# Three scatter tables in place of one, and an earlier routing queue, in an attention and mixture-of-experts kernel

## The chip, the cores and the metric

The kernel runs on one core of a Trainium2 chip. The metric is device time in microseconds, the median of several executions. The engines are TensorE (PE; PEld is its loading of weights), VectorE (DVE), ScalarE (ACT), GpSimd (POOL) and SyncE (SP), each with a queue of its own that is worked in order. GpSimd issues the indirect DMAs (gathers and scatters by a list of addresses) and the stores of attention outputs, SyncE the plain loads.

## What is computed

Windowed attention for 8 batches of 8 heads, 576 positions each (half the heads look back 32 positions, half 128 positions in steps of 4), then a mixture of 8 experts with one expert for each of 4608 tokens:

```python
x = attention(q, k, v).transpose(0, 2, 1, 3).reshape(4608, 512)
logits = x @ w_gate                       # 8 experts
expert_idx = argmax(logits, axis=1)
gate_w = softmax(logits)[arange, expert_idx]
for e in range(8):
    mask = expert_idx == e
    out[mask] = gate_w[mask, None] * (maximum(x[mask] @ w1[e], 0) @ w2[e])
```

## The kernel before

**Attention** runs over 36 steps, each a block of 128 rows; nine steps are a pair of batches (`NPR = 4` pairs, numbered 0 to 3 here and called first to last in the text). `step(n)` issues the scores of block n (L264), the transposed probabilities of n-1, the output of n-2 (L311), the normalised rows `xs` (L331, three buffers), their two or three stores to `x_d` on GpSimd (L343, L353), the transposed rows of n-3 and the router's logits of n-4. Loads of queries, keys and values run three to five steps ahead on SyncE, six buffers each.

**Routing** (`route(m)`) is called once a pair. It puts its operations into the list `side`, from which `pull_off` takes one at five places of a step, and `pull_pe` those for TensorE, if at least `GAP` pulls have gone by since the last one or the step is `FREE` or later. It picks the expert by argmax (`mx`, `sh`, `cand`, `fst`, `oh`), counts ranks with three matmuls (`rank`), and makes for each token a slot in a table of 40960 integers, held by expert and then by place; `at_i` is the slot's address. `scatter` (L502) then writes the tokens' row numbers to the table `t_d` in device memory by nine indirect DMAs of 128 integers. As all write the one tensor, each waits for the one before.

The first two pairs (`EARLY = 2`) are enough for two blocks of expert 0: `early_fetch` reads two columns of the table into `row_i` (L616), gathers 2 x 128 rows (L683), and `turn_x` (L731) transposes them in later attention steps. After the third pair the whole table is read into `tbl`. The last pair needs no scatter: `mark` makes two one-hot tiles for each of nine blocks (`s1`, L514, and `b1`, L523; every third `b1` on GpSimd), `enter` multiplies them on TensorE into `tb` (L534), and `row_i = tbl + scr` (L603) is the whole list of rows. The stretch from the last attention step to the first gathers with it is called the seam.

**Experts**: 8 static blocks of 4 x 128 rows, and dynamic blocks for what is left, split float32 matmuls in two layers (L771, L802), weights loaded by SyncE and GpSimd and split by ScalarE and VectorE (L657, L658).

**Order.** For steps 0 to 34 (`MEND = 35`) TensorE, VectorE and ScalarE keep the order of the code; later steps, GpSimd and SyncE are ordered by the scheduler of the framework, which also sets the waits between engines. Which work a step holds is set by `at(n, ...)`: route(m) is due after step 13, 22, 31 (five after the pair's last block) and 39.

Of the kernel before, what the change touches and what calls it, by code (L numbers as in the profile page):

```python
# [9 lines left out]
F32 = mybir.dt.float32  # L10
F32R = mybir.dt.float32r
I32 = mybir.dt.int32
BF16 = mybir.dt.bfloat16
AF = mybir.ActivationFunctionType
ALU = mybir.AluOpType
# [9 lines left out]
DM = H * DH  # L25
NE = 8
DF = 1024
P = 128
# [4 lines left out]
NPR = B // 2  # L33
S2 = 2 * S
NT = S2 // P
# [8 lines left out]
NBK = NE * BPE  # L44
# [4 lines left out]
DUMMY = P  # L49
# [5 lines left out]
EB = 2  # L55

NTHR = 40
NWARM = 9
GAP, FREE = 4, 31

# [8 lines left out]
def _constants():  # L69
    c = np.zeros((P, C_ALL), np.float32)  # L70
# [25 lines left out]
    end = row[:, -1].astype(np.float32) - LAST  # L96
    slots = np.repeat(np.arange(P, dtype=np.int32), NBK).reshape(P, NBK)

# [9 lines left out]
    mask = mask.astype(mybir.dt.np(BF16))  # L108
    return dict(cst=c, tok=tok, end=end, slots=slots, mask=mask, zero=np.zeros((DUMMY, DM), np.float32))

# [37 lines left out]
@with_exitstack  # L148
def attention_moe_kernel(ctx, tc, qk, v, wg, w, cst, tok, end, slots, mask, zero, out):
    nc = tc.nc  # L150
# [6 lines left out]
    g_d = dram.tile([N + DUMMY, 1], F32, name="g_d")  # L157
    t_d = dram.tile([P * NBK, 1], I32, name="t_d")

    cc = const.tile([P, C_ALL - C_ATT], F32, name="cc")  # L160
    ident = const.tile([P, P], F32, name="ident")
    crun = const.tile([P, NE], F32, name="crun")
    tbl = const.tile([P, NBK], I32, name="tbl")
    scr = const.tile([P, NBK], F32, name="scr")
# [53 lines left out]
    def load_rest():  # L218
        nc.sync.dma_start(cc, cst[:, C_ATT:])
        nc.sync.dma_start(rows_i, tok)  # L220
        nc.sync.dma_start(rows_f, end)
        nc.sync.dma_start(t_d[:].rearrange("(p b) o -> p (b o)", p=P), slots)

# [190 lines left out]
    def off_pe(f, *a, **k):  # L414
        side.append((0, lambda: f(*a, **k)))
# [16 lines left out]
    def route(m, then=None, after=None):  # L432


        v = nc.vector
        lgs = lgts[m]
        box = {}

# [18 lines left out]
        def small(name, shape=(P, NT, NE), dt=F32):  # L457
            return sp.tile(list(shape), dt, name=name, bufs=1)
# [6 lines left out]
        ]  # L465
        pos, blk_i, plc_i, at_i = [
            small(n, (P, NT), I32) for n in ("pos", "blk_i", "plc_i", "at_i")
        ]
# [25 lines left out]
        def gate_out():  # L494
            nc.scalar.copy(gts, box["gt"])
            taken[0] = False
            lo = DUMMY + m * S2
            nc.sync.dma_start(g_d[lo : lo + S2].rearrange("(t p) o -> t (p o)", p=P), gts)

        def scatter(ts):  # L500
            for t in ts:
                nc.gpsimd.indirect_dma_start(  # L502
                    out=t_d[:],
                    out_offset=bass.IndirectOffsetOnAxis(ap=at_i[:, t : t + 1], axis=0),
                    in_=rows_i[:, m, t : t + 1],
                    in_offset=None,
                )
# [3 lines left out]
        def mark(t):  # L511
            s1 = sp.tile([P, P], F32R, name="s1", bufs=6)
            b1 = sp.tile([P, NBK], F32R, name="b1", bufs=6)
            v.tensor_scalar(  # L514
                s1,
                ca[:, C_IO - C_TRI : C_IO + P - C_TRI],
                plc[:, t : t + 1],
                pay[:, t : t + 1],
                op0=ALU.is_equal,
                op1=ALU.mult,  # L520
            )
            e = v if t % 3 else nc.gpsimd
            e.tensor_scalar(  # L523
                b1, cc[:, C_BK - C_ATT : C_BK + NBK - C_ATT], blk[:, t : t + 1], None, op0=ALU.is_equal
            )
            hot[t] = s1, b1
# [43 lines left out]
        off_pe(v.tensor_copy, pos, posf)  # L570
        off_pe(v.tensor_scalar, blk_i, pos, -P, None, op0=ALU.bitwise_and)
        if m < NPR - 1:
            off_pe(v.tensor_scalar_mul, wide, posf, float(NBK))
            off_pe(
# [11 lines left out]
        else:  # L586
            off_pe(v.tensor_scalar, plc_i, pos, P - 1, None, op0=ALU.bitwise_and)
            off_pe(v.tensor_copy, blk, blk_i)
# [24 lines left out]

    def read_table(to, n):

        nc.sync.dma_start(to[:, :n], t_d[:].rearrange("(p b) o -> p (b o)", p=P)[:, :n])  # L616

# [364 lines left out]
    def at(n, f, *a):  # L982
        todo.setdefault(n, []).append(lambda: f(*a))

    turning = []

    def early_fetch():
        def fetch():
            at(now[0] + 1, read_table, row_i, EB)
            at(now[0] + 2, first.fetch_x)  # L990
            for i in range(EB):
                at(now[0] + 3 + 2 * i, turning.append, i)

        off_pe(fetch)

    def early_gates():
        off_pe(lambda: at(now[0] + 2, first.fetch_gates))
        reserve()

    now = [0]  # L1000
    for m in range(NPR):
        last = (m + 1) * NT - 1 + (4 if m == NPR - 1 else 5)
        if m == EARLY - 1:
            at(last, route, m, early_fetch, early_gates)
        elif m == NPR - 2:
            at(last, route, m, lambda: off_pe(read_table, tbl, NBK))
        else:
            at(last, route, m)
# [332 lines left out]
_HOST = ["q", "k", "v", "moe_w_gate", "moe_w1", "moe_w2"]  # L1341
_ARGS = ["qk", "v", "wg", "w", "cst", "tok", "end", "slots", "mask", "zero"]

# [22 lines left out]
```

## Time and profile before

| | |
|---|---|
| median of 3 runs | 692.63 us (690.27 to 693.84) |
| profiled execution | 692.2 us, of it 690.2 us span |
| TensorE busy | 622.8 us, 90% |
| VectorE busy | 355.7 us, 52% |
| ScalarE busy | 308.3 us, 45% |
| GpSimd busy | 276.8 us, 40% |

TensorE is the engine that sets the time over most of the span; the question for a change is where it isn't busy. "Idle before" of a row is the time in which the engine had nothing to run just ahead of it, with the engine or transfer that ended it. The granted clock of TensorE is given as a share of full speed, which has two levels, 1.2 and 2.4 GHz; a stretch between them is a mixture.

### The profile page before, as it was taken

How to read it: one execution, taken by the hardware profiler on the slowest of the kernel's cores; microseconds unless marked ns; L12 is line 12 of the kernel's file. 1: busy time of each engine (PE TensorE's matmuls, PEld its weight loads, DVE VectorE, ACT ScalarE, POOL GpSimd, SP SyncE). 2: the span in 40 equal slices, each digit the busy share in tenths (PEclk: the TensorE clock that was granted, in tenths of full speed). 3: DMA queues.
4: the chain of work that ended last, by engine and by line, in shares of the span. 5: the costliest groups of instructions: out<-in, count | busy, mean ns of one | idle time of the engine just before them, and what ended most of it. 6: DMA issues, size and time to landing. Idle time of an engine off the chain costs nothing. (4 is left out here: it accounts for less than half of the span.)

```text
span 690.2 us, 13243 instructions
## 1 busy us (share of the span) xinstructions
PE 622.8 (90%) x5231; PEld 497.8 (72%) x5231; DVE 355.7 (52%) x756; ACT 308.3 (45%) x610; POOL 276.8 (40%) x316
## 2 busy tenths in 40 slices
PE   7999996794296889999999999999999999999991
PEld 6777775673275767888888878878887888778781
DVE  3877874574064694656445635744563661361210
ACT  2676673373072343555445535633553551351100
POOL 0333333566454564413630661473165155323220
PEclk8999999799599799999999999999999999999996
DMA  8999997782221355737627744663764465454310
GB/s 330 409 411 399 369 340 235 220 267 85 76 70 40 94 193 180 240 114 246 209 94 239 232 155 145 218 215 85 252 214 153 168 223 208 143 213 156 115 43 32
DMA packets 42183, 135.09 MB, mean 196 GB/s; under 512 B 9204, under 2 KB 10136, under 8 KB 42072
## 3 DMA queue, kind: packets, MB, share of 16 engines
q1 hardware_dynamic: 21608, 75.72, 31.1%
q0 software_dynamic: 20512, 58.51, 25.6%
q8 instruction: 42, 0.69, 0.4%
q14 instruction: 21, 0.17, 0.1%
HBM read 114.91 MB, written 19.99 MB: 195 GB/s over the span
## 5 line engine op out<-in xcount | busy, mean ns | idle before, releaser
L771 PE MATMUL hps<-x,wu 128*128 128x512 f32 (+1 forms) x720 | 168.7, 390 | 3.2 <-DVE h L783 2.8
L658 DVE TENSOR_TENSOR wu<-raw,wu 128x512 fp32r<-128x512 f32 x200 | 128.6, 687 | 80.0 <-ACT wu L657 76.8
L802 PE MATMUL yps<-wu,h 128*128 128x512 f32 x696 | 166.7, 394 | 0.0
L771 PEld LDWEIGHTS hps<-x,wu 128*128 128x128 f32 x720 | 134.0, 191 | 32.4 <-DVE h L783 4.0
L802 PEld LDWEIGHTS yps<-wu,h 128*128 128x128 f32 x696 | 129.8, 188 | 29.7 <-issue 0.6
L657 ACT CAST wu<-raw 128x512 fp32r<-128x512 f32 x200 | 113.0, 618 | 82.3 <-DMA raw<-in_w_dram,wi 39.2
L703 POOL DMA_INDIRECT out_dram<-y,row_i x32 | 35.1, 1096 | 136.2 <-DVE y L702 88.2
L301 ACT COPY pts<-pt 96x512 f32<-96x512 f32 x72 | 42.0, 583 | 89.0 <-PE pt L296 78.3
L783 DVE SCALAR_TENSOR_TENSOR h<-hps,h 128x512 fp32r<-128x512 f32 (+1 forms) x60 | 39.5, 669 | 76.4 <-ACT h L782 68.5
L782 ACT ACTIVATE h<-hps 128x512 fp32r<-128x512 f32 (+1 forms) x60 | 34.2, 582 | 95.9 <-PE hps L771 72.1
L835 POOL DMA_INDIRECT raw<-in_w_dram,wi x40 | 42.6, 1066 | 41.8 <-DVE wu L658 30.9
L275 DVE TENSOR_REDUCE nm<-s 128x4 f32<-128x384 f32 x72 | 39.5, 549 | 35.0 <-PE s L264 32.3
L683 POOL DMA_INDIRECT xg<-x_d,row_i x32 | 33.8, 1056 | 50.9 <-PE tpx L826 25.0
L311 PE MATMUL o<-vr,pts 96*64 96x65 f32 x1152 | 43.3, 230 | 8.2 <-DVE xs L331 8.1
L296 PE MATMUL pt<-ident,p 128*96 128x128 f32 x288 | 48.9, 295 | 1.6 <-ACT pts L301 1.6
L343 POOL DMA_DIRECT2D x_d<-xs x36 | 20.7, 574 | 71.8 <-DVE xs L331 38.8
L311 PEld LDWEIGHTS o<-vr,pts 96*64 96x64 f32 x1152 | 38.2, 142 | 15.6 <-DVE xs L331 9.1
L883 PE MATMUL ypd<-wu,hd 128*128 128x512 f32 x168 | 46.5, 415 | 0.3 <-ACT hd L872 0.3
L502 POOL DMA_INDIRECT t_d<-rows_i,at_i x27 | 27.4, 1014 | 47.3 <-DMA t_d<-rows_i,at_i 38.4
L702 DVE TENSOR_SCALAR y<-yps,gate 128x256 f32<-128x256 f32 x30 | 14.4, 481 | 56.1 <-ACT y L701 56.1
L280 DVE TENSOR_TENSOR d<-s,nm 128x384 f32<-128x384 f32 x72 | 40.0, 557 | 4.8
L701 ACT ACTIVATE y<-yps,gate 128x256 f32<-128x256 f32 x30 | 14.2, 473 | 62.5 <-PE yps L802 58.7
(160 smaller groups left out, 766.3 us busy)
## 6 DMA issues: line engine op xcount, KB each, us to landing
raw<-in_w_dram SPq DMA_DIRECT2D x64, 512.0 KB, 4.9
qkr<-in_qk_dram SPq DMA_DIRECT2D x36, 576.0 KB, 8.1
vr<-in_v_dram SPq DMA_DIRECT2D x36, 520.0 KB, 5.4
x_d<-xs POOLq DMA_DIRECT2D x44, 128.0 KB
x_d<-xs POOLq DMA_DIRECT2D x8, 112.0 KB
x_d<-xs POOLq DMA_DIRECT2D x8, 96.0 KB
x_d<-xs POOLq DMA_DIRECT2D x8, 80.0 KB
raw<-in_w_dram,wi POOLq DMA_INDIRECT x40
```

The source lines that it names most:

```text
L275: nc.vector.tensor_reduce(st["nm", n][:, g], st["s", n][g], axis=AX.X, op=ALU.max)
L280: nc.vector.tensor_tensor(st["d", n][:, g], st["s", n][g], st["nm", n][:, g].broadcast_to([P, HP, KB]), op=ALU.subtract,)
L296: nc.tensor.transpose(pt[:KB, h], st["p", n][:, g, h], ident)
L301: nc.scalar.copy(st["pts", n][:, g], st.pop(("pt", n))[:KB])
L311: nc.tensor.matmul(st["o", n][QB * j : QB * (j + 1), g, h], lhsT=pts[:, g, h, QB * j : QB * (j + 1)], rhs=vr[:KB, n % NRV, a : a + DH + 1] ...
L657: nc.scalar.copy(u[:, 0, sl], raw[:, sl])
L658: nc.vector.tensor_tensor(u[:, 1, sl], raw[:, sl], u[:, 0, sl].bitcast(F32), op=ALU.subtract)
L771: nc.tensor.matmul(hps[:, : self.ns], lhsT=u[:, wpart, fs], rhs=self.x[:, xpart, c, : self.ns], start=(k == 0), stop=(k == 11),)
L783: nc.vector.scalar_tensor_tensor(h[:, 1, :n], hps[:, :n], 0.0, h[:, 0, :n].bitcast(F32), op0=ALU.max, op1=ALU.subtract,)
L802: nc.tensor.matmul(yps, lhsT=self.h[f][:, hpart, ts], rhs=u[:, wpart, fs], start=(k == 0), stop=(k == 23),)
L835: nc.gpsimd.indirect_dma_start(out=raw, out_offset=None, in_=w, in_offset=bass.IndirectOffsetOnAxis(ap=self.wi[:, u : u + 1], axis=0),)
L883: nc.tensor.matmul(yps, lhsT=self.h[f // 4][:, hpart, f % 4], rhs=u[:, wpart, fs], start=(k == 0), stop=(k == 23),)
```

## The change

- There are three tables, `tabs`, cleared to zero; the scatter of block t goes to table t % 3, and what it writes is `rel_i`, the row number less the place in the block (`plc_i`), so that an empty slot is zero.
- Reading is three DMAs into `tbl`, `scr` and `none` (`read_table`), and `add_tables` adds them and the place, two VectorE operations. For the early read the addition and the gathers are due three steps after the step that takes the last scatter from the list; before, the gathers were due two steps after it.
- All `b1` one-hots of the last pair are on VectorE, and the copy of each pair's gates goes from ScalarE to VectorE.
- The routing of the first three pairs is due one step earlier (after steps 12, 21 and 30), `GAP` is 3 in place of 4, `FREE` 35 in place of 31, and the first TensorE operation of a routing waits for the gap too.

```diff
-GAP, FREE = 4, 31
+GAP, FREE = 3, 35
...
-    t_d = dram.tile([P * NBK, 1], I32, name="t_d")
+    tabs = [dram.tile([P * NBK, 1], I32, name=f"tab{i}") for i in range(3)]
...
-        nc.sync.dma_start(t_d[:].rearrange("(p b) o -> p (b o)", p=P), slots)
+        for tab in tabs:
+            nc.sync.dma_start(
+                tab[:].rearrange("(p b) o -> p (b o)", p=P), zero[:, :NBK].bitcast(I32)
+            )
...
+        ticks[1] = ticks[0] - 1
...
-            nc.scalar.copy(gts, box["gt"])
+            v.tensor_copy(gts, box["gt"])
...
-                    out=t_d[:],
+                    out=tabs[t % 3][:],
                     out_offset=bass.IndirectOffsetOnAxis(ap=at_i[:, t : t + 1], axis=0),
-                    in_=rows_i[:, m, t : t + 1],
+                    in_=rel_i[:, t : t + 1],
...
-            e = v if t % 3 else nc.gpsimd
-            e.tensor_scalar(
+            v.tensor_scalar(
...
+        off_pe(v.tensor_scalar, plc_i, pos, P - 1, None, op0=ALU.bitwise_and)
         if m < NPR - 1:
+            off_pe(v.tensor_tensor, rel_i, rows_i[:, m], plc_i, op=ALU.subtract)
...
-    def read_table(to, n):
-
-        nc.sync.dma_start(to[:, :n], t_d[:].rearrange("(p b) o -> p (b o)", p=P)[:, :n])
+    parts = [tbl, scr, none]
+
+    def read_table(n):
+
+        for tab, to in zip(tabs, parts):
+            nc.sync.dma_start(
+                to[:, :n].bitcast(I32), tab[:].rearrange("(p b) o -> p (b o)", p=P)[:, :n]
+            )
+
+    def add_tables(to, n):
+
+        t0, t1, t2 = [t[:, :n] for t in parts]
+        nc.vector.scalar_tensor_tensor(
+            t0,
+            t0.bitcast(I32),
+            cc[:, C_P - C_ATT : C_P + 1 - C_ATT],
+            t1.bitcast(I32),
+            op0=ALU.add,
+            op1=ALU.add,
+        )
+        nc.vector.tensor_tensor(to[:, :n], t0, t2.bitcast(I32), op=ALU.add)
...
+    def read_all():
+        off_pe(read_table, NBK)
+        off_pe(add_tables, tbl, NBK)
+
     def early_fetch():
         def fetch():
-            at(now[0] + 1, read_table, row_i, EB)
-            at(now[0] + 2, first.fetch_x)
+            at(now[0] + 1, read_table, EB)
+            at(now[0] + 3, add_tables, row_i, EB)
+            at(now[0] + 3, first.fetch_x)
             for i in range(EB):
-                at(now[0] + 3 + 2 * i, turning.append, i)
+                at(now[0] + 4 + 2 * i, turning.append, i)
...
-        last = (m + 1) * NT - 1 + (4 if m == NPR - 1 else 5)
+        last = (m + 1) * NT - 1 + 4
```

The order of instructions shows what moves. GpSimd, at the scatters of the first pair, before (x_d rows are the stores of attention outputs; the names behind "waits" are counters of other engines and of GpSimd's own eight DMA counters in turn, the first of them mostly that of the DMA eight before, a second one that of the scatter waited for):

```order
L502 DMA t_d<-rows_i,at_i 40960x1 [waits DMAHW0_49,DMAHW2_49,DMASW0_49,DVE_49]
L343 DMA x_d<-xs 128x256 [waits DMASW1_49,DVE_49]
L353 DMA x_d<-xs 128x256 [waits DMASW2_49]
L502 DMA t_d<-rows_i,at_i 40960x1 [waits DMASW3_49,DMASW0_49]
L502 DMA t_d<-rows_i,at_i 40960x1 [waits DMASW4_49,DMASW3_49]
L343 DMA x_d<-xs 128x256 [waits DMASW5_49,DVE_49]
L353 DMA x_d<-xs 128x256 [waits DMASW6_49]
L502 DMA t_d<-rows_i,at_i 40960x1 [waits DMASW7_49,DMASW4_49]
```

and the same place of the changed kernel:

```order
L505 DMA tab_65<-rel_i,at_i 40960x1 [waits DMAHW2_49,DMASW0_49,DVE_49]
L505 DMA tab_66<-rel_i,at_i 40960x1 [waits DMAHW3_49,DMASW1_49]
L505 DMA tab_67<-rel_i,at_i 40960x1 [waits DMAHW4_49,DMASW2_49]
L505 DMA tab_65<-rel_i,at_i 40960x1 [waits DMASW3_49,DMASW0_49]
L505 DMA tab_66<-rel_i,at_i 40960x1 [waits DMASW4_49,DMASW1_49]
L505 DMA tab_67<-rel_i,at_i 40960x1 [waits DMASW5_49,DMASW2_49]
L345 DMA x_d<-xs 128x256 [waits DMASW6_49,DVE_49]
L355 DMA x_d<-xs 128x256 [waits DMASW7_49]
L505 DMA tab_65<-rel_i,at_i 40960x1 [waits DMASW3_49]
```

Each scatter waited for the one before; now it waits for the third before, and six stand ahead of the next store in place of one.

VectorE in the seam, before, from the gathered logits of the last pair (`lt`) on:

```order
L453 TENSOR_REDUCE lt<-tl 128x24 x2
L415 TENSOR_REDUCE mx<-lt 128x9
L542 TENSOR_TENSOR sh<-lt,mx 128x72
L544 SCALAR_TENSOR_TENSOR cand<-sh,ca 128x72
L546 TENSOR_REDUCE fst<-cand 128x9
```

and in the changed kernel:

```order
L456 TENSOR_REDUCE lt<-tl 128x24 x2
L629 SCALAR_TENSOR_TENSOR tbl<-tbl,cc,scr 128x320
L804 SCALAR_TENSOR_TENSOR x<-s,x 128x256
L456 TENSOR_REDUCE lt<-tl 128x24
L417 TENSOR_REDUCE mx<-lt 128x9
L637 TENSOR_TENSOR tbl<-tbl,none 128x320
L544 TENSOR_TENSOR sh<-lt,mx 128x72
L546 SCALAR_TENSOR_TENSOR cand<-sh,ca 128x72
L548 TENSOR_REDUCE fst<-cand 128x9
```

The two additions over the whole tables have moved in between the operations of the last pair's routing.

SyncE, from the last loads of attention on, in the changed kernel (before, one read `row_i<-t_d` and one `tbl<-t_d` stood there):

```order
L196 DMA vr<-in_v_dram 128x1040 x2
L772 DMA raw<-in_w_dram 128x1024
L622 DMA tbl<-tab_65 128x2
L501 DMA g_d<-gts 9x128
L622 DMA scr<-tab_66 128x2
L622 DMA none<-tab_67 128x2
L196 DMA vr<-in_v_dram 128x1040
L772 DMA raw<-in_w_dram 128x1024 x3
L622 DMA tbl<-tab_65 128x320
L622 DMA scr<-tab_66 128x320
L501 DMA g_d<-gts 9x128
L622 DMA none<-tab_67 128x320
```

Each read has become three, with one load of values and weights behind the first three.

## Rows read from the trace of the kernel before

**Rows 1.** Busy time by stage: length, then busy and count by engine, clock, DMA.

```profile
core 0: us, PE busy (x) PEld busy (x) DVE busy (x) ACT busy (x) POOL busy (x), PEclk, DMA share, GB/s
...
18.50:98.20 79.70, 79.70 (x1547) 61.80 (x1546) 62.58 (x156) 53.96 (x115) 29.17 (x52) 1.00 1.01 387
98.20:152.10 53.90, 43.56 (x744) 33.04 (x742) 30.20 (x82) 28.30 (x62) 28.02 (x40) 0.91 0.77 250
152.10:197.00 44.90, 21.22 (x342) 16.52 (x341) 15.26 (x41) 14.87 (x32) 22.63 (x27) 0.77 0.27 89
...
270.00:677.40 407.40, 403.70 (x1991) 325.73 (x1989) 194.12 (x317) 177.24 (x333) 152.78 (x147) 1.00 0.53 175
```

**Rows 2.** Timeline of TensorE: scores of steps 13, 22, 26, 27, 31, 35.

```profile
59.43 0.89 PE L264 MATMUL s<-qkr 64*64 64x96 f32 x32
...
98.24 0.89 PE L264 MATMUL s<-qkr 64*64 64x96 f32 x32
...
124.41 1.37 PE L264 MATMUL s<-qkr 64*64 64x96 f32 x32
...
130.28 0.89 PE L264 MATMUL s<-qkr 64*64 64x96 f32 x32
...
152.11 0.89 PE L264 MATMUL s<-qkr 64*64 64x96 f32 x32
...
197.01 0.89 PE L264 MATMUL s<-qkr 64*64 64x96 f32 x32
```

**Rows 3.** Timeline of all engines: the two long waits in attention.

```profile
119.22 0.69 DVE L331 TENSOR_TENSOR xs<-o,rz 128x512 f32<-128x512 f32 x1 [7.50 <-DMA x_d<-xs]
...
179.70 0.33 SPq L616 DMA_DIRECT2D row_i<-t_d  x1
182.25 1.00 POOL L683 DMA_INDIRECT xg<-x_d,row_i  x1 [4.95 <-DMA row_i<-t_d]
...
185.83 1.08 PE L731 MATMUL tpx<-ident,xg 128*128 128x128 f32 x4 [20.52 <-DMA xg<-x_d,row_i]
```

**Rows 4.** Timeline of GpSimd: scatters, a weight subtraction, a gather.

```profile
101.09 1.01 POOL L502 DMA_INDIRECT t_d<-rows_i,at_i  x1 [4.45 <-DMA t_d<-rows_i,at_i]
...
166.84 1.28 POOL L672 TENSOR_TENSOR wu<-raw,wu 128x512 fp32r<-128x512 f32 x1
...
170.78 0.97 POOL L502 DMA_INDIRECT t_d<-rows_i,at_i  x1 [1.46 <-DMA t_d<-rows_i,at_i]
...
183.56 0.98 POOL L683 DMA_INDIRECT xg<-x_d,row_i  x1 [0.30 <-issue]
...
204.54 0.99 POOL L502 DMA_INDIRECT t_d<-rows_i,at_i  x1 [2.86 <-DMA t_d<-rows_i,at_i]
```

**Rows 5.** Timeline of all engines in the seam.

```profile
198.42 0.17 DVE L415 SCALAR_TENSOR_TENSOR at_i<-blk_i,wide 128x9 int32<-128x9 int32 x1
...
214.04 0.23 DVE L542 TENSOR_TENSOR sh<-lt,mx 128x72 f32<-128x72 f32 x1
...
217.40 0.38 DVE L523 TENSOR_SCALAR b<-cc,blk 128x320 fp32r<-128x320 f32 x1
...
219.83 0.38 DVE L523 TENSOR_SCALAR b<-cc,blk 128x320 fp32r<-128x320 f32 x1
...
226.13 0.64 PE L534 MATMUL tb<-b,s 128*128 128x320 f32 x1 [8.11 <-POOL b L523]
...
234.95 0.48 DVE L415 TENSOR_TENSOR row_i<-tbl,scr 128x320 int32<-128x320 int32 x1
...
240.10 0.66 PE L826 MATMUL tpx<-ident,xg 128*128 128x128 f32 x4 [0.61 <-DMA xg<-x_d,row_i]
```

**Rows 6.** Page, groups: the first store of each attention output.

```profile
L343 POOL DMA_DIRECT2D x_d<-xs x36 | 20.7, 574 | 71.8 <-DVE xs L331 38.8
```

**Rows 7.** Page, DMA issues: loads of values, median to landing.

```profile
vr<-in_v_dram SPq DMA_DIRECT2D x36, 520.0 KB, 5.4
```

More of the change, by code (lines that the diff above doesn't have):

```diff
@@ L96, in _constants @@
     end = row[:, -1].astype(np.float32) - LAST
-    slots = np.repeat(np.arange(P, dtype=np.int32), NBK).reshape(P, NBK)
     t, p, w = np.meshgrid(np.arange(NT), np.arange(P), np.arange(KB), indexing="ij")
@@ L108, in _constants @@
     mask = mask.astype(mybir.dt.np(BF16))
-    return dict(cst=c, tok=tok, end=end, slots=slots, mask=mask, zero=np.zeros((DUMMY, DM), np.float32))
+    return dict(cst=c, tok=tok, end=end, mask=mask, zero=np.zeros((DUMMY, DM), np.float32))
 def _layout(q, k, v, wg, w1, w2):
@@ L148, in attention_moe_kernel @@
 @with_exitstack
-def attention_moe_kernel(ctx, tc, qk, v, wg, w, cst, tok, end, slots, mask, zero, out):
+def attention_moe_kernel(ctx, tc, qk, v, wg, w, cst, tok, end, mask, zero, out):
     nc = tc.nc
@@ L162, in attention_moe_kernel @@
     crun = const.tile([P, NE], F32, name="crun")
-    tbl = const.tile([P, NBK], I32, name="tbl")
+    tbl = const.tile([P, NBK], F32, name="tbl")
     scr = const.tile([P, NBK], F32, name="scr")
@@ L465, in route @@
         ]
-        pos, blk_i, plc_i, at_i = [
-            small(n, (P, NT), I32) for n in ("pos", "blk_i", "plc_i", "at_i")
+        pos, blk_i, plc_i, at_i, rel_i = [
+            small(n, (P, NT), I32) for n in ("pos", "blk_i", "plc_i", "at_i", "rel_i")
         ]
@@ L586, in route @@
         else:
-            off_pe(v.tensor_scalar, plc_i, pos, P - 1, None, op0=ALU.bitwise_and)
             off_pe(v.tensor_copy, blk, blk_i)
@@ L985, in attention_moe_kernel @@
     turning = []
+    def read_all():
+        off_pe(read_table, NBK)
+        off_pe(add_tables, tbl, NBK)
     def early_fetch():
         def fetch():
-            at(now[0] + 1, read_table, row_i, EB)
-            at(now[0] + 2, first.fetch_x)
+            at(now[0] + 1, read_table, EB)
+            at(now[0] + 3, add_tables, row_i, EB)
+            at(now[0] + 3, first.fetch_x)
             for i in range(EB):
-                at(now[0] + 3 + 2 * i, turning.append, i)
+                at(now[0] + 4 + 2 * i, turning.append, i)
         off_pe(fetch)
     def early_gates():
-        off_pe(lambda: at(now[0] + 2, first.fetch_gates))
+        off_pe(lambda: at(now[0] + 3, first.fetch_gates))
         reserve()
@@ L1005, in attention_moe_kernel @@
         elif m == NPR - 2:
-            at(last, route, m, lambda: off_pe(read_table, tbl, NBK))
+            at(last, route, m, read_all)
         else:
@@ L1341 @@
 _HOST = ["q", "k", "v", "moe_w_gate", "moe_w1", "moe_w2"]
-_ARGS = ["qk", "v", "wg", "w", "cst", "tok", "end", "slots", "mask", "zero"]
+_ARGS = ["qk", "v", "wg", "w", "cst", "tok", "end", "mask", "zero"]
 def kernel(**inputs):
```

## The prediction

> **What bounds the kernel now.** I read the busy time by stage first, then the start of every attention step on TensorE, then the longest waits, then the queue of GpSimd, and last the seam where attention hands over to the experts.
>
> By stage [rows 1] TensorE is never idle from 18.5 to 98.2 us, and nearly never from 270 to 677.4 us (403.7 of 407.4 us busy). Between them it is not: 43.6 of 53.9 us busy, then 21.2 of 44.9 us, and in both the granted clock is below one. So whatever shortens 98 to 240 us moves the rest forward as it is, and nothing else in the change can pay.
>
> The step starts [rows 2] give the undisturbed pace. From step 13 (59.43) to step 22 (98.24) nine steps and the routing of one whole pair take 38.81 us, 4.31 us a step. The next nine take 53.87 us (152.11), and the four after that 44.90 us (197.01) where four undisturbed ones would take 17.2. That is 42.7 us over the pace in 13 steps.
>
> The waits name the cause [rows 3]. At 119.22 VectorE had waited 7.5 us for an attention output buffer whose store to memory was stuck on GpSimd's queue. At 185.83 TensorE had been idle 20.52 us in front of the transposes of the first expert's rows: their gather waited for the table (read issued at 179.70, gather at 182.25), and the read waited for the last of 18 scatters. The scatters are chained [rows 4]: each goes to the same table and waits for the one before. With loads streaming, GpSimd stood 4.45 us behind a scatter of 1.02 us, a pitch of 5.47 us; with the queues quiet 1.46 us behind one, 2.48 us; near the end of attention 2.86, or 3.88 us. Two gathers to different tiles follow each other with 0.30 us between, so a pitch near 1.3 us is what GpSimd can issue.
>
> **The change part by part.** *Three tables.* Scatter t now waits for scatter t-3 only, as the order of GpSimd in the section on the change shows. Nine scatters become three rounds. I take the loaded 5.47 us for a round, as loads still stream when they run: 16.4 us instead of nine pitches, 49 us. The Trainium skill ("DMA: Bandwidth & Descriptors", section on the anatomy of one DMA on the gpsimd path) puts the fixed cost of such a DMA at about 2.0 us, whatever the load; with the 1.02 us of issue that is 3 us a round. The quiet pitch agrees with it, the loaded one doesn't, and I go by the loaded one.
>
> First pair, steps 13 to 22 and beyond: the nine scatters are out in about 14 us, GpSimd's stores of attention outputs stand behind at most six scatters (some 8 us), and an output buffer comes round again after three steps (12.9 us at the pace). The wait of 7.5 us and the smaller ones after it mostly go. I leave 1.2 us of them; 0 and 4 are the bounds. Steps 22 to 31 then take 38.81 + 1.2 = 40.0 us, step 31 starts at 138.3 instead of 152.11: a gain of 13.9 us. In it lie the half-speed steps after each idle stretch: the scores of step 26 (124.41) took 1.37 us, and that step, to 130.28, 5.87 us, some 1.5 over the pace [rows 2]. The gates' copies on VectorE instead of ScalarE are a part of the pace and cost nothing: one short copy each, on an engine with slack.
>
> Second pair: here the chain is still the one that ends last. Its first scatter leaves about 6 us after the start of step 27 (the addresses are the third routing operation of that step). Three rounds, 16.4 us, follow, and two subtractions of weights of 1.28 us [rows 4] stand between scatters on GpSimd; the rounds have room for about half of them, so 1.5 us. Then the last scatter's own landing is included in the third round, and three small reads follow, 2.55 us as the one at 179.70 took [rows 3]. The sum of tables is possible some 27 to 29 us after the start of step 27; I take 28.5, with the stores of step 26 wedged in. What was a wait of TensorE for the gather becomes a wait of VectorE: the two additions stand ahead of the maxima of step 32, which VectorE would begin five steps (21.6 us) and about 1 us for the scores after step 27. So VectorE stands for 28.5 - 22.6, about 6 us, with all of attention behind it on that engine, and TensorE follows through the scores' buffers. I price it at 6.5 us and the lower clock after it at 1.5 us (as in step 26). Bounds: at the quiet pitch the chain is 9 us shorter and the wait is gone; at 7 us a round it is 4.6 us longer. SyncE stands in front of the reads meanwhile, but all loads of queries and keys are ahead of them; only one load of values (needed at step 37) and weights are behind.
>
> Steps 31 to 35 then cost 17.2 + 0.7 (one transposition of gathered rows that the pace doesn't hold; 1.08 at the lower clock [rows 3]) + 6.5 + 1.5 = 25.9 us. Step 35 starts at 138.3 + 25.9 = 164.2 instead of 197.01: **32.8 us gained**.
>
> *The seam.* Before, the third pair's addresses were ready 1.4 us after the scores of step 35; its table is read late, and nothing waits for it. The last pair's chain ran: first operation after the maxima at 214.04, one-hots from 217.40, first product with them at 226.13 after TensorE had waited 8.11 us for two one-hots that GpSimd had behind its scatters, the row list at 234.95, the first transposes of gathered rows at 240.10, 43.1 us after step 35 [rows 5]. Now GpSimd's one-hots go to VectorE. From 217.40 to 219.83 nine starts took 2.43 us, so 18 cost 18 x 0.27 = 4.9 us, and the 8.11 us go. But two things are put in front. The third pair's ranking now stands behind the scores of step 35, not ahead of them: its addresses come one step later, 1.4 + 4.3 + 0.7, about 6.5 us after step 35. And the addition of the three tables stands on VectorE inside the last pair's chain. Nine scatters at 1.3 us and five stores at 0.57 us between them [rows 6] are 14.6 us; the last lands 3.9 - 1.3 us later, at +23.7; the read of a whole table (160 KB) lies between the small one, 2.55 us, and a 520 KB load, 5.4 us [rows 7], say 3.4: +27.1. VectorE would have been there at +17, so it waits 10 us. From there as before: 3.4 us to the one-hots, 4.9 us of them, 0.5 us to the last product, then the 3.1 us of passes over the sum, the row list at +39, against +38.4 before (234.95 + 0.48). The one-hots' gain is eaten by the tables: **0.6 us lost**, between 5 lost (loaded pitch, slow reads) and 4.5 gained (quiet pitch).
>
> *Small things.* Two more tables to clear are 320 KB more on queues full from 18.5 to 98.2 us, but TensorE didn't stand once there. Four VectorE operations more a pair, under 0.2 us each, lie in VectorE's slack (62.6 of 79.7 us busy [rows 1]). From 270 us on nothing changes.
>
> **Sum.** The profiled execution took 692.2 us (span 690.2, 2.0 around it), 0.4 below the median, so no correction. 692.2 - 32.8 + 0.6 = **660.0**.
>
> **The rivals.** (1) *The quiet pitch holds even under load*: rounds of 2.5 to 3 us. Then VectorE never waits at the additions of step 31 (8.0 us more gained), the first pair's rest goes (1.2) and the seam gains up to 3: 660 - 12, about 648. For it: the quiet rows, and the page's 2 us. Against it: the loaded rows are of just this stage. By that page's figure this is the case that comes.
> (2) *Scatters in flight slow each other*: three at once take about 11 us a round. The second pair's chain ends 16 us later, on VectorE, the seam 5: about 681. For it: all go through one queue, among stores and loads. Against it: gathers issued 1.3 us apart show no wait for each other.
> (3) *They don't overlap at all*, in that the queue finishes one scatter before it starts the next. This is the case that ends slower. The chains are then as long as before and attention gains nothing but the gates' copies (some 3 us); in the seam, nine scatters at 3.88 us from +6.5 end at +41.4, the read at +44.8, the row list at +56.7 where it was +38.4: 18 lost, 692 - 3 + 18, about 707. Attention gaining only 3 us, it decides against the change once the row list comes later than +41.4, which is when the nine take over some 20 us in the seam. Against it: the same rows of gathers.
> That the change doesn't do what it says (waits still on the one before) is shut out by the order of GpSimd.
>
> **How the numbers follow.** My forecast 0.78, rival 1 0.11, rival 2 0.07, rival 3 0.04. Its own range: 660 less 8.0, 1.2 and 3 is 648, plus 4.6, 2.8 and 4.5 is 672. That holds most of rival 1 and leaves out the other two, so the range is 647 to 672. A measurement of this kernel can tell about 0.5% (3.5 us) from no change: faster 0.95, the same 0.01, slower 0.04.
>
> **What would show it.** Right: step 22 still near 98 and step 31 near 138; scatters 1.3 us apart in threes with some 2.5 us between the threes; one idle stretch of 4 to 9 us on VectorE ahead of the table's addition near 143 us; step 35 near 164; in the seam VectorE idle about 10 us ahead of the second addition and no wait for one-hots; the stage from the first gathered rows to the end as long as now. Wrong: step 31 well past 140 (stores still starve buffers), scatters over 6 us a round, or a seam that differs from 43 us by over 5.

## The result and the profile after

The changed kernel takes 671.8 us (median of four runs, 668.6 to 675.0) beside 691.8 for the one before: a ratio of 0.971, 95% interval 0.965 to 0.976. That is faster, and 0.2 us inside the stated range of 647 to 672, but 20 us are gained where 32 were forecast. The profiled execution took 671.0 us, of it 669.0 us span. Busy time by stage, with stages cut where the pace changes (columns as in [rows 1]):

```profile
core 0: us, PE busy (x) PEld busy (x) DVE busy (x) ACT busy (x) POOL busy (x), PEclk, DMA share, GB/s
18.50:89.70 71.20, 71.20 (x1385) 55.26 (x1383) 55.11 (x139) 47.99 (x102) 27.55 (x50) 1.00 1.02 397
89.70:106.14 16.44, 12.31 (x166) 7.94 (x165) 7.71 (x21) 7.03 (x15) 10.10 (x14) 0.90 0.71 226
106.14:136.60 30.46, 30.12 (x578) 23.79 (x577) 24.07 (x67) 20.39 (x45) 12.80 (x22) 1.00 0.93 326
136.60:149.20 12.60, 10.25 (x170) 7.24 (x169) 6.41 (x18) 7.01 (x15) 9.90 (x12) 1.00 0.64 199
149.20:173.20 24.00, 21.19 (x340) 16.53 (x339) 16.41 (x39) 14.33 (x30) 18.31 (x23) 0.86 0.55 177
```

TensorE is busy nearly all the time from 106 to 137 us, where the kernel before stood for output buffers [rows 1, 3]. But two stretches are new: 89.7 to 106.1, steps 20 and 21, take 16.4 us where the pace of 4.31 us gives 8.6, and 136.6 to 149.2, steps 29 and 30, take 12.6. In both the loads fall to 226 and 199 GB/s from 397. At these times the scatters of the first and the second pair are in flight. The first of the two stretches in the timeline of all engines, the rows that matter here (start, duration, engine, line; in brackets the idle time before and what ended it; "remote" is a signal that the profile can't trace to an instruction):

```profile
87.28 1.16 PE L313 MATMUL o<-vr,pts 96*64 96x65 f32 x32
87.72 1.04 POOL L505 DMA_INDIRECT tab<-rel_i,at_i  x1 [0.30 <-DVE nm L277]
88.36 0.64 PE L298 MATMUL pt<-ident,p 128*96 128x128 f32 x4
89.06 0.99 POOL L505 DMA_INDIRECT tab<-rel_i,at_i  x1 [0.30 <-issue]
89.70 0.56 PE L266 MATMUL s<-qkr 64*64 64x96 f32 x16
90.36 0.96 POOL L505 DMA_INDIRECT tab<-rel_i,at_i  x1 [0.30 <-issue]
90.45 0.40 PE L266 MATMUL s<-qkr 64*64 64x96 f32 x4 [0.19 <-issue]
91.18 0.42 PE L266 MATMUL s<-qkr 64*64 64x96 f32 x5 [0.33 <-issue]
91.19 0.33 SPq L196 DMA_DIRECT2D vr<-in_v_dram  x1
91.20 0.17 DVE L323 TENSOR_SCALAR z<-o 128x8 f32<-128x8 f32 x1 [2.10 <-remote]
91.92 0.58 ACT L303 COPY pts<-pt 96x512 f32<-96x512 f32 x1 [3.83 <-remote]
91.93 0.45 PE L266 MATMUL s<-qkr 64*64 64x96 f32 x7 [0.34 <-issue]
92.39 0.96 POOL L505 DMA_INDIRECT tab<-rel_i,at_i  x1 [1.07 <-DMA tab<-rel_i,at_i]
```

The scatters run as meant: three 1.3 us apart, then a wait for the first of them to land. TensorE's output `o` was done at 88.44 and its transposes `pt` at 89.00, by the ends that the profile gives them (it models the ends of TensorE's products). Yet VectorE, which needs the one, went on at 91.20, ScalarE, which needs the other, at 91.92, and SyncE's next load of values, which follows the end of `o` by 0.04 us elsewhere, came at 91.19. TensorE itself broke off in the middle of a group that waits for nothing and trickled, four to seven products every 0.7 us. Then all went on together. All late signals here are TensorE's, and as the loads of values wait for one of them, the loads fall too. The same comes back with later trios. Below, such a stretch is called a stall.

The early addition and the seam:

```profile
154.96 0.20 DVE L629 SCALAR_TENSOR_TENSOR tbl<-tbl,cc,scr 128x2 f32<-128x2 int32 x1
155.64 2.23 DVE L637 TENSOR_TENSOR row_i<-tbl,none 128x2 int32<-128x2 f32 x1 [0.48 <-DMA none<-tab]
...
173.17 0.89 PE L266 MATMUL s<-qkr 64*64 64x96 f32 x32
...
198.06 0.55 DVE L629 SCALAR_TENSOR_TENSOR tbl<-tbl,cc,scr 128x320 f32<-128x320 int32 x1 [5.89 <-DMA scr<-tab]
199.00 0.80 PE L792 MATMUL hps<-x,wu 128*128 128x256 f32 x2 [5.47 <-DVE x L804]
...
212.76 0.48 DVE L417 TENSOR_TENSOR row_i<-tbl,scr 128x320 int32<-128x320 f32 x1
...
218.50 0.60 PE L847 MATMUL tpx<-ident,xg 128*128 128x128 f32 x4
```

The 20.52 us in front of the first gathered rows [rows 3] are gone, and so are the 8.11 us for GpSimd's one-hots [rows 5]; in their place VectorE waits 5.9 us for the whole table and TensorE 5.5 us behind it.

### The profile page after: what moved, and what is told of

The parts are those of the page before. It is cut to its first block, busy times and chain, and to the rows that moved or that the text cites. A ratio compares the mean times of both kernels' runs of the same rounds, so it can differ in the third digit from the quotient of the medians.

```text
span 669.0 us, 13272 instructions
## 1 busy us (share of the span) xinstructions
PE 627.9 (94%) x5231; PEld 499.8 (75%) x5231; DVE 360.6 (54%) x773; ACT 308.0 (46%) x606; POOL 271.9 (41%) x313
## 5 line engine op out<-in xcount | busy, mean ns | idle before, releaser
L856 POOL DMA_INDIRECT raw<-in_w_dram,wi x40 | 41.3, 1033 | 41.5 <-DVE wu L679 26.3
L313 PE MATMUL o<-vr,pts 96*64 96x65 f32 x1152 | 44.8, 228 | 3.3 <-issue 3.1
L904 PE MATMUL ypd<-wu,hd 128*128 128x512 f32 x168 | 46.5, 415 | 0.3 <-ACT hd L893 0.3
L292 ACT ACTIVATE p<-d 128x384 f32<-128x384 f32 x72 | 37.6, 525 | 8.4 <-DVE d L282 8.4
```

The lines of the kernel that those rows point to most:

```text
L313: nc.tensor.matmul(st["o", n][QB * j : QB * (j + 1), g, h], lhsT=pts[:, g, h, QB * j : QB * (j + 1)], rhs=vr[:KB, n % NRV, a : a + DH + 1] ...
L856: nc.gpsimd.indirect_dma_start(out=raw, out_offset=None, in_=w, in_offset=bass.IndirectOffsetOnAxis(ap=self.wi[:, u : u + 1], axis=0),)
L904: nc.tensor.matmul(yps, lhsT=self.h[f // 4][:, hpart, f % 4], rhs=u[:, wpart, fs], start=(k == 0), stop=(k == 23),)
```

## The experiments

All kernels compute the whole result. Starts of steps on TensorE are in us from the span's start; the seam is the time from the scores of step 35 to the first transposes of the dynamic blocks' rows (L826 before, L847 after). The ratio is to the kernel before as it ran beside each of them (690.5 to 693.9 us); probe_count, below, ran once.

| kernel | median, us | ratio to before | step 22 | step 31 | step 35 | seam |
|---|---|---|---|---|---|---|
| before | 691.8 | | 98.2 | 152.1 | 197.0 | 43.1 |
| changed | 671.8 | 0.971 (0.965 to 0.976) | 106.1 | 149.2 | 173.2 | 45.3 |
| one_table | 688.1 | 0.996 (0.992 to 0.999) | 98.2 | 149.5 | 187.7 | 44.5 |
| two_tables | 673.7 | 0.976 (0.974 to 0.978) | 98.0 | 145.4 | 177.1 | 41.5 |
| old_order | 661.6 | 0.957 (0.954 to 0.961) | 98.4 | 140.0 | 161.8 | 47.4 |
| after_again | 670.9 | 0.969 (0.963 to 0.975) | 101.5 | 147.1 | 171.5 | 45.8 |
| later | 670.7 | 0.967 (0.961 to 0.974) | 99.7 | 145.6 | 170.0 | 43.0 |
| gap4 | 669.7 | 0.967 (0.960 to 0.973) | 104.7 | 145.7 | 172.7 | 43.9 |
| onehot | 670.9 | 0.968 (0.963 to 0.974) | 105.6 | 147.9 | 174.9 | 46.1 |
| shift | 675.1 | 0.974 (0.969 to 0.978) | 107.0 | 150.1 | 171.5 | 45.3 |
| filler | 670.4 | 0.968 (0.965 to 0.972) | 106.1 | 149.2 | 172.4 | 44.2 |
| spread0 | 667.2 | 0.963 (0.959 to 0.967) | 98.7 | 147.6 | 169.5 | 45.8 |
| old_late | 661.0 | 0.954 (0.950 to 0.959) | 100.3 | 141.5 | 163.4 | 45.2 |

### Is it the trios, the order, or the place?

The first question was whether the stall comes from three scatters in flight (A), from the new routing order (B), or sits at its place in the program (C).

*one_table* and *two_tables*: the changed kernel with fewer tables.

```diff
-    tabs = [... for i in range(3)]
+    tabs = [... for i in range(1)]      # two_tables: range(2), and add_tables sums so many
...
-                    out=tabs[t % 3][:],
+                    out=tabs[0][:],             # two_tables: tabs[t % 2]
```

> The changed kernel with one table again, all else kept (earlier routing, VectorE's one-hots and copies). Theory A: the missing 11 us are lost because three small scatters in flight at once hold up the signals between engines and the loads for 2 to 3 us a trio. Then no trio, no such stall: step 22 starts near 99 us instead of 106, no waits of VectorE and ScalarE for a remote signal; but the chain is serial, so the early addition waits some 25 to 30 us and the seam some 15 us: step 35 near 197, the whole 695 to 712 us. Theory B: the earlier and denser routing queue and VectorE's extra operations cost the time, whatever the tables: step 22 stays near 106 and the whole is above 705. Theory C: the stall belongs to the place in the program (its code being loaded): stall at step 20 as in the changed kernel.

> The changed kernel with two tables. Theory A (three in flight hold up signals and loads): at most two in flight, so the stall is under half: step 22 near 100 to 102 us. The chain of the second pair is five rounds instead of three, some 24 us: the early addition waits about 8 us, the seam 8 us more than with three; the whole 674 to 684 us. Theory B (order of routing): step 22 stays near 106 us, the whole 682 to 690. Theory C (place in the program): step 22 near 106 too.

With one table and with two, step 22 starts at 98.2 and 98.0 us, and no engine waits for a remote signal. The whole came out shorter than theory A had it, 688.1 us for 695 to 712 and 673.7 for 674 to 684. In two_tables (rows of the stretch shown above) the load of values follows the end of `o` at once:

```profile
86.94 1.16 PE L313 MATMUL o<-vr,pts 96*64 96x65 f32 x32
87.38 1.04 POOL L505 DMA_INDIRECT tab<-rel_i,at_i  x1 [0.30 <-DVE nm L277]
88.14 0.33 SPq L196 DMA_DIRECT2D vr<-in_v_dram  x1
88.73 0.98 POOL L505 DMA_INDIRECT tab<-rel_i,at_i  x1 [0.30 <-issue]
89.36 0.89 PE L266 MATMUL s<-qkr 64*64 64x96 f32 x32
93.44 0.95 POOL L505 DMA_INDIRECT tab<-rel_i,at_i  x1 [3.73 <-DMA tab<-rel_i,at_i]
```

The order is that of the changed kernel in all three. That looks as if B and C had fallen, but these executions differ in more than their tables. one_table, two_tables, old_order and probe_count ran side by side, the others at other times, and the profiles of these four differ from all ten others where nothing was changed. Near the end of the experts GpSimd gathers weights, 1.25 us apart, while TensorE makes `hpt`, for which ScalarE waits; the kernel before, then two_tables:

```profile
649.19 1.93 PE L938 MATMUL hpt<-wu,xt 128*32 128x256 f32 x32
653.14 0.39 ACT L945 ACTIVATE ht<-hpt 128x256 f32<-128x256 f32 x1 [3.24 <-remote]
...
628.90 1.93 PE L958 MATMUL hpt<-wu,xt 128*32 128x256 f32 x32
630.90 0.38 ACT L965 ACTIVATE ht<-hpt 128x256 f32<-128x256 f32 x1 [1.30 <-PE hpt L958]
```

In the kernel before, with one table, the signal of `hpt` comes 2.0 us after its end, in two_tables 0.1. This wait is 1.30 us in the four and 3.2 to 3.3 us, for a remote signal, in the ten others. From 15 us on the four have no wait for a remote signal of over 0.5 us, and each of the ten has three or more of over 1 us. So there are two sorts of executions: in one TensorE's signals come late now and then, in the other they don't. The profiles of the changed kernel are of the first sort, those of one_table and two_tables of the second. That the stall is missing from these two can therefore come from the sort of execution, and their waits settle neither A nor B nor C. The medians stand, as each is compared with the kernel before that ran beside it (690.5 us beside the four, 691.8 to 693.9 beside the others).

What fewer tables lose is the chain: VectorE's longest wait in attention's second half is

```profile
DVE row_i L629 <- DMA tbl<-tab: 19.9, 1, 19.9
```

with one table and 13.3 us with two. One table with all the rest of the change gains 0.4%, so without the tables the rest is worth next to nothing.

*old_order*: three tables, routing queued as before.

```diff
-GAP, FREE = 3, 35
+GAP, FREE = 4, 31
...
-        ticks[1] = ticks[0] - 1
...
-        last = (m + 1) * NT - 1 + 4
+        last = (m + 1) * NT - 1 + (4 if m == NPR - 1 else 5)
```

> The changed kernel with three tables and VectorE's one-hots, but the routing queue as in the kernel before (due one step later, gap of 4, free from step 31 on). Theory A (trios in flight): the stalls move one step later with the scatters and stay as long: steps 13 to 31 take 88 to 91 us as in the changed kernel (89.6), and some 3 trios of stalls each for the first and the second pair; the whole 668 to 676 us. Theory B (order of routing): steps 13 to 31 take 79 to 82 us and the whole is 658 to 664 us. Theory C: the stall stays at the place in the program, steps 20 to 22.

This is B's number: 661.6 us, steps 13 to 31 in 80.2 us, no wait for a remote signal, and trios as close as in the changed kernel.

```profile
92.16 1.02 POOL L504 DMA_INDIRECT tab<-rel_i,at_i  x1 [0.30 <-DVE d L282]
93.48 1.00 POOL L504 DMA_INDIRECT tab<-rel_i,at_i  x1 [0.30 <-issue]
93.73 0.89 PE L266 MATMUL s<-qkr 64*64 64x96 f32 x32
94.79 0.96 POOL L504 DMA_INDIRECT tab<-rel_i,at_i  x1 [0.30 <-issue]
```

Three scatters start within 2.6 us here too, and TensorE runs on. So a trio is not enough for the stall; whether the order or the sort of execution makes the difference this run can't tell.

*probe_count* was to show the stall away from routing, by scatters to scratch tables in the steps before it.

```diff
+    todo[6] = [lambda: small_rows(0, 1)]    # one scatter
+    todo[8] = [lambda: small_rows(1, 2)]    # two, to two tables
+    todo[10] = [lambda: small_rows(3, 3)]   # three, to three tables
```

> The changed kernel with extra scatters of 128 integers to scratch tables that nobody reads, in the undisturbed steps before any routing: one after step 6, two to two tables after step 8, three to three tables after step 10. Theory A: after one no gap in TensorE, after two under 1 us, after three an idle stretch of 2 to 3 us in TensorE in which VectorE and ScalarE wait for remote signals, and little moved by the loads meanwhile; step 13 some 2 to 4 us later than in the changed kernel (59.6). Theories B and C: TensorE stays busy through all of them, step 13 at most 0.5 us later.

It missed its aim: the framework put all six in a row (35.19 to 41.62 us), behind a wait of VectorE of 3.4 us for the constants that their addresses need; step 12 starts 3.5 us late (58.42 for 54.93), no more than that wait. No remote wait came with the six, nor with both pairs' own trios, which are in the order of the changed kernel but those 3.5 us later: step 22 at 101.8, which is 98.3 + 3.5. As the sort of execution has no late signals, that says nothing against A.

It says something else: this is the changed order without the stall, and it is no faster. The one execution took 674.0 us, 670.5 without the 3.5. Waits that the stalled executions don't have are back (VectorE):

```profile
113.61 0.69 DVE L333 TENSOR_TENSOR xs<-o,rz 128x512 f32<-128x512 f32 x1 [3.28 <-DMA x_d<-xs]
...
155.09 0.60 DVE L629 SCALAR_TENSOR_TENSOR tbl<-tbl,cc,scr 128x2 f32<-128x2 int32 x1 [5.55 <-DMA scr<-tab]
155.74 0.16 DVE L637 TENSOR_TENSOR row_i<-tbl,none 128x2 int32<-128x2 f32 x1
```

In step 24 (8.8 us) VectorE waits for an output buffer whose store is late, at 155.09 for the tables. For an output buffer it waits 5.6 us in old_order and 8.4 in two_tables as well (in two waits each), and not at all in the profiles of the changed kernel, after_again, shift and filler, where steps 20 to 22 stall. That the stall gave the stores this time is my reading.

### Is it an accident, and which half of the order?

> The changed kernel once more, unaltered, beside the next two. Theory D: the waits for remote signals and the trickling TensorE at steps 20 to 22 (8 us) and 27 to 30 (3 us) belong to this order of work, since the kernel with the old routing order has none and starts step 22 at 98.4 us: then this run shows them at the same places, step 22 near 106, the whole 669 to 675 us. Theory E: they are an accident of one execution or chip: then step 22 starts near 98 us, and the whole is 658 to 664 us.

> The changed kernel with one thing of the old order: the routing of the first three pairs due one step later; the gap of 3, step 35 and the counting from the start stay. Theory D1: the step at which the scatters come decides (they meet the loads otherwise): step 22 near 98.4 us, the whole 659 to 664 us as with the whole old order. Theory D2: the denser routing queue (gap 3) decides: a stall of some 8 us at steps 21 to 23, the whole 668 to 675 us. Theory E: 659 to 664 us.

> The changed kernel with the other half of the old order: a gap of 4, free from step 31 on, no counting from the start; the routing stays due one step earlier. Theory D1 (the step of the scatters decides): step 22 near 106 us, the whole 668 to 675 us. Theory D2 (the denser queue decides): step 22 near 98.4 us, the whole 657 to 664 us. Theory E: 657 to 664 us.

after_again is the changed kernel itself; *later* has only the change of `last`, *gap4* only the other two lines of old_order. after_again gives 670.9 us and shows the stalls again; they lie a step apart (steps 20 to 22 take 19.4 us in all where three at the pace take 12.9), so this is no accident of one execution. Late signals don't need scatters either. In after_again TensorE's scores, done at 157.63, reach VectorE 2.7 us later:

```profile
156.74 0.89 PE L266 MATMUL s<-qkr 64*64 64x96 f32 x32
160.29 0.56 DVE L277 TENSOR_REDUCE nm<-s 128x4 f32<-128x384 f32 x1 [2.62 <-remote]
```

The second pair's tables have been read and added by then; what GpSimd issues there, 1.3 us apart, are the early gathers. filler (2.71 us) and gap4 (2.30 us) have the same wait at the same gathers.

*later* and *gap4* give 670.7 and 669.7 us, with remote waits in both, so D1 and D2 both fall (gap4's own numbers are D1's, but *later* misses D1's total): neither half alone brings the 10 us of the two together. In *later* step 22 comes at 99.7, and the loss moves to step 30 (8.3 us) and steps 33 and 34.

### Late code, or close scatters?

*shift* moves TensorE's code by some 100 instructions, *filler* was to space the scatters of the first two pairs.

```diff
-NWARM = 9
+NWARM = 2
...
+    for i in range(32):
+        nc.tensor.matmul(warm_ps[:32, :1], lhsT=cold[:, :32], rhs=cold[:, :1], start=True, stop=True)
```

> The changed kernel with other warm-up products of TensorE at the start: 2 large ones and 32 tiny ones in place of 9 large ones, which moves the rest of TensorE's code by some 100 instructions and changes no order. Theory F: the trickle of TensorE (4 to 5 products every 0.72 us without any wait) is its own code arriving late while scatters are in flight: with the code cut elsewhere the stalls move or go, step 22 starts before 100 us or the stall lies in another step, the whole differs from 671 us by over 4 us. Theory G (scatters hold up the signals, wherever the code lies): trickle and late signals again from 2.5 us after the first scatter on, step 22 at 105 to 108 us, the whole 668 to 675 us.

> The changed kernel with a fill of 128x512 floats by GpSimd behind each scatter of the first two pairs, so that scatters start some 1.7 to 2.3 us apart instead of 1.3 and fewer are in flight. Theory G (three scatters within 2.6 us hold up signals): no waits for remote signals in steps 19 to 22, step 22 starts at 98 to 100 us; the second pair's chain is 3 to 8 us longer, the early addition waits for it; step 35 at 168 to 172 and the whole 663 to 670 us. Theory F or another place-bound cause: step 22 stays near 106 us, the whole 672 to 680 us.

In shift steps 20 and 21 take 16.1 us (16.4 in the changed kernel), and the trickle begins as late behind the first scatter as there: F in this form falls, though the two steps share the loss otherwise (10.8 and 5.3 us for 7.9 and 8.6) and the median, 675.1, is 0.1 above G's range. filler tells nothing, because GpSimd's fills depend on nothing and were all issued before 11 us; the scatters kept their 1.3 us, and the run is one more of the changed kernel (670.4 us, step 22 at 106.1).

*spread0* does what filler was meant to, for the first pair alone, by a copy that depends on the addresses.

```diff
+                at_t = at_i[:, t : t + 1]
+                if m == 0:
+                    ix = sp.tile([P, 448], I32, name="ix", bufs=3)
+                    nc.gpsimd.tensor_copy(ix, at_t.broadcast_to([P, 448]))
+                    at_t = ix[:, :1]
...
-                    out_offset=bass.IndirectOffsetOnAxis(ap=at_i[:, t : t + 1], axis=0),
+                    out_offset=bass.IndirectOffsetOnAxis(ap=at_t, axis=0),
```

> The changed kernel with GpSimd's scatters of the first pair alone spread out: ahead of each GpSimd copies its addresses over 448 columns (some 1.5 us by the 1.08 us that 320 columns took), so that never three of them start within 2.6 us; the second pair stays as it is, three tables for both. Theory G (three scatters started within 2.6 us hold up the signals): no wait for a remote signal and no trickling products in steps 19 to 23, step 22 at 98 to 100 us; in the second pair, with its scatters 1.3 us apart, the trickle is back; the stores behind the longer chain cost up to 4 us in steps 23 to 26, the whole 662 to 669 us. If the number of tables alone decides (three transfers outstanding, however far apart): late signals again, step 22 at 104 us or later, the whole above 670 us.

The first pair, then the second, in the timeline:

```profile
87.98 1.05 POOL L510 DMA_INDIRECT tab<-rel_i,ix  x1 [0.18 <-POOL ix L508]
89.33 0.98 POOL L510 DMA_INDIRECT tab<-rel_i,ix  x1 [0.30 <-issue]
91.16 0.98 POOL L510 DMA_INDIRECT tab<-rel_i,ix  x1 [0.28 <-POOL ix L508]
98.65 0.89 PE L266 MATMUL s<-qkr 64*64 64x96 f32 x32
...
132.38 1.02 POOL L510 DMA_INDIRECT tab<-rel_i,at_i  x1 [0.30 <-DVE nm L277]
134.78 0.89 PE L266 MATMUL s<-qkr 64*64 64x96 f32 x32
135.00 1.03 POOL L510 DMA_INDIRECT tab<-rel_i,at_i  x1 [0.18 <-issue]
136.17 0.68 PE L313 MATMUL o<-vr,pts 96*64 96x65 f32 x14
136.33 0.95 POOL L510 DMA_INDIRECT tab<-rel_i,at_i  x1 [0.30 <-issue]
137.04 0.39 PE L313 MATMUL o<-vr,pts 96*64 96x65 f32 x5 [0.19 <-issue]
138.55 0.56 DVE L277 TENSOR_REDUCE nm<-s 128x4 f32<-128x384 f32 x1 [3.63 <-remote]
139.31 0.58 ACT L303 COPY pts<-pt 96x512 f32<-96x512 f32 x1 [2.78 <-remote]
141.68 1.56 PE L266 MATMUL s<-qkr 64*64 64x96 f32 x32
```

The first pair, spread: no remote wait, step 22 at 98.65 as G has it. The second: late signals, the trickle, and step 29 takes 6.9 us. But G's bound falls. The first trio starts within 3.2 us (87.98 to 91.16) and does no harm; the second pair's stall begins with three scatters within 4.0 us (132.38, 135.00, 136.33). Spreading took the first stall away, in one execution of the sort that has late signals; a rule in microseconds it isn't. The median is 667.2 us; the profiled execution, 674.0, is the longest of the four and took 6.4 us more from the first gathered rows to the end than the changed kernel's. The 7.5 us won at step 22 shrink to 3.6 at step 35: stores hold the output buffers again, and one step (23) takes 9.3 us.

### Two attempts at a better kernel

*onehot* has no scatter in attention.

```diff
-            for lo in range(0, NT, 2):
-                off_pe(scatter, range(lo, min(lo + 2, NT)))
+            for lo in range(0, NT + 3, 3):
+                if lo < NT:
+                    off_pe(lambda lo=lo: [mark(t) for t in range(lo, lo + 3)])
+                if lo:
+                    on_pe(enter, range(lo - 3, lo), late=True)
...
```

> A version without any scatter in attention: every pair makes its piece of the table as the last pair does, one-hot tiles (the 128-column ones by VectorE, the 320-column ones by GpSimd) multiplied on TensorE and added in VectorE to the table; the queue's gap is 2. TensorE gets 27 products of 0.31 to 0.47 us more, 8 to 13 us; in exchange no chain, no table reads, no wait at an early addition, no wait for the table in the seam. Sum: step 22 at 98.4 + 3.5 = 102, step 31 at 144, step 35 at 163, the first transposes of gathered rows 41 to 43 us later, the whole 653 to 660 us. Rival: GpSimd's one-hots (1.1 us each before) slow VectorE through their shared memory port, and TensorE's products stand in front of scores: step 22 past 106, the whole above 668 us.

Its rival came: no remote wait anywhere in routing, but step 22 at 105.6 and 670.9 us. GpSimd's one-hots take 1.07 us each, and TensorE stands for them (2.8 us in four waits) with the next scores behind. In the experts a signal is late here too: ScalarE waits 4.12 us at 233.81 while GpSimd issues five gathers and scatters 1.2 to 1.4 us apart, and TensorE keeps its pace of 0.23 us a product. This kernel has no scatter to a table at all.

*old_late* takes the wait for the whole table out of old_order's seam.

```diff
-        off_pe(add_tables, tbl, NBK)
...
+            # last pair, behind its one-hots; pcol is made from the last of them
+            off_pe(add_tables, tbl, NBK, pcol)
```

> Three tables with the old routing order (661.6 us) and one thing more: in the seam the addition of the three tables, for which VectorE waited 6.7 + 1.8 us with the last pair's whole chain behind it, is moved behind the last pair's one-hot tiles (by a column operand made from the last of them), so that VectorE goes on without the table. Theory: the seam's wait is what is left of the scatters on the path: 6 to 8 us less, 654 to 656 us. Rival: what is late next takes its place at once (the last pair's own chain of TensorE and VectorE work, or weights): 659 to 662 us.

The wait of 6.7 us for the table is gone, but the seam is only 2.2 us shorter (45.2 for 47.4), and onehot, which reads no table at all, has 46.1: what is late next is the last pair's own chain. At 661.0 us (658.1 to 667.5) it can't be told from old_order. Its profile is of the sort with late signals, and one trio costs a short trickle in it (step 22 at 100.3): steps 13 to 22 take 40.4 us, where the executions of the changed kernel, after_again, shift and filler take 42.4 to 46.5. So the old order lessens the stall and doesn't shut it out. old_order and old_late both beat the changed kernel by some 10 us.

## Why the prediction was right, and where it was short

That 671.8 lies inside the range is luck: it does so by 0.2 us, and the range reaches that far for rounds of up to 7 us, which took 4.7 to 5.2, for output buffers and for a slow seam, while most of the loss came from a cost that no term had. The profiled execution took 11.0 us more than the forecast 660.0. By the forecast's own steps:

1. **Steps 13 to 22, "step 22 still near 98": failed, 7.9 us.** It started at 106.14. I priced the scatters only by their chain and by the stores behind them on GpSimd, and put their price for TensorE, its signals and the loads at nothing. No rival held this either: "scatters in flight slow each other" was about the rounds, and those were not slowed.
2. **Steps 22 to 31, 40.0 us: 43.0, and 3.0 us lost for the same reason.** From 106.14 to 136.62 seven steps take 4.35 us each, without a wait for an output buffer; then steps 29 and 30 stall. That the shorter chain alone frees the buffers, as I had it, isn't borne out: where the stall is missing the waits are back, and these nine steps take 41.6 us in old_order, 43.3 in probe_count. The 1.2 us that I left for them were too few.
3. **The scatter chain: about right.** Nine left in 13.2 us (forecast 14); rounds took 4.67 and 4.94 us in the first pair, near the loaded 5.47 us that I took [rows 4]. The estimate of 3 us a round that follows from the Trainium skill's fixed cost ("DMA: Bandwidth & Descriptors", the anatomy of one DMA on the gpsimd path) did not come under load; the trace decides.
4. **The early addition: place right, wait wrong.** The sum was possible 27.9 us after the start of step 27 (127.70 to 155.64; forecast 28.5). VectorE stood 0.5 us for it and not 6.5, for it came late itself, after the stalls of point 2. In probe_count, without them, it came as forecast: 28.3 us after the start of step 27 (127.46 to 155.74), with VectorE waiting 5.6 us. Steps 31 to 35 took 24.0 for 25.9 us: 1.9 us back.
5. **The seam: 45.3 for 43.7 us, 1.6 lost.** VectorE waited 5.9 us for the table, not 10; the row list came at +40.1 for +39. No one-hot was waited for.
6. **From there to the end: 450.5 us, before 450.1**, 0.4 lost.

Together 7.9 + 3.0 - 1.9 + 1.6 + 0.4 = 11.0. So in this execution the missing gain is points 1 and 2. But it would not have come back with the stall gone. probe_count, less its 3.5 us, is 10.5 us over the forecast as well, by other terms: 3.3 in steps 22 to 31 (output buffers), 1.8 in steps 31 to 35, 1.4 in the seam and 3.8 behind it, all in one execution. The stall and the priced waits stand in for each other. Between the two executions in which no signal is late, probe_count and old_order, the largest difference is in steps 31 to 35, 27.7 beside 21.8 us, so the price of the new order isn't the stall alone.

old_order, with the same tables, lies near the forecast: step 22 at 98.4, step 31 at 140.0 (138.3), step 35 at 161.8 (164.2), 661.6 us (660.0). It does so in part because errors cancel: steps 31 to 35 took 21.8 us for 25.9, the seam 47.4 for 43.7.

Shown: three tables under the old order beat the changed kernel by some 10 us, in two sets of runs (old_order 0.957, old_late 0.954, the changed kernel 0.971 and 0.969). In executions with late signals the stall comes again at the close scatters of these kernels (changed kernel, after_again, later, gap4, shift, filler, second pair of spread0). In executions of the same sort the kernel before, with its chained scatters, and onehot, with none, have no such wait in attention, and spreading the first pair's scatters removed the first stall in the unchanged order. It begins early: `o`'s signal of 88.44 fails to come when only the first scatter, of 87.72, has started; the second starts at 89.06.

Not shown: that the number of tables decides, since one and two tables ran only in executions without late signals. Late signals also come with gathers and in kernels without a trio. What makes an execution one of the one sort or the other is open, and whether the recording of the profile takes part in it, and with it how much executions without a profile stall. What holds the signals is open too.

## What to carry to other kernels

A chain of small scatters is worth cutting into several tables. Try such a change apart from any reordering that comes with it: here tables and one-hots under the old order gave 29 us (661.6 beside 690.5), and under the new order some 20. Compare the pace of the bottleneck engine in the very stretch, before and after; a loss there can hide another wait, so taking it away may pay far less than its length. And before a wait in one execution is put down to a change in the kernel, look at a stretch that the change doesn't touch: if the two executions differ there too, the comparison shows the execution and not the kernel.

## What the runs showed of the hardware that I had not expected

In some executions TensorE's signals came 2 to 4 us late to other engines while GpSimd issued indirect DMAs 1.2 to 1.3 us apart, scatters of 128 integers or gathers alike (VectorE waited 2.10 us, ScalarE 3.83 in the changed kernel; 2.0 us late at `hpt` in the kernel before). At the close scatters TensorE also trickled, four to seven products every 0.7 us without a wait of its own, and the loads fell from 397 to 226 GB/s. In other executions, with the same gathers at the same pace, the signal of `hpt` came within 0.1 us.
